# The last output projections as block products, with wo's sums on GpSimd and the first gate and up weights loaded earlier

## The chip, the cores and the metric

The kernel runs on one core of one Trainium2 chip. The metric is the device time of one execution in microseconds (us). The kernel before has a median of 749.18 us over three runs (748.45 to 749.22).

## The reference

x is 2048 tokens by 1024 features, all tensors are bf16. It is normalised, goes through a linear attention block and a SwiGLU block, and the two are joined as x + s * silu(f).

```python
xn = _layernorm(x, axis=-1)
# linear attention, 32 heads of 32
q, k, v = split_heads(xn @ wqkv)
phi = lambda t: jnp.where(t > 0, t + 1, jnp.exp(t)) + 1e-6
pq, pk = phi(q), phi(k)
kv = jnp.einsum("bhsd,bhse->bhde", pk, v)
z = jnp.einsum("bhsd->bhd", pk)
o = jnp.einsum("bhqd,bhde->bhqe", pq, kv) / (jnp.einsum("bhqd,bhd->bhq", pq, z)[..., None] + 1e-6)
s = merge_heads(o) @ wo
# SwiGLU, inner width 3584
f = (silu(xn @ w_gate) * (xn @ w_up)) @ w_down
return x + s * silu(f)
```

## The kernel before, in words

All matrix products take 128 partitions and 512 moving columns at a time. There are four stages on TensorE's queue.

1. The front (to 154 us of the span): normalisation, transposes, keys, values, most of the queries, and the sums kvz over the tokens.
2. The output stage (154 to 233 us), in which the change lies. The 2048 tokens are 4 blocks (b) of 4 tiles (t) of 128 tokens. For each tile `emit_ND` multiplies pqT (phi of the queries, one tile for each pair of feature groups) with KVZ, eight matmuls of 132 columns into three PSUM buffers of pool psA; VectorE adds to the denominators (L794), inverts them (L797) and multiplies (L800) into o_sb. `emit_OT` writes o_sb to HBM from ScalarE's queue and reads it back transposed from SyncE's (SP's) queue into oT; blocks 0 and 1 have oT of their own (`oT_ab`), blocks 2 and 3 lie in wq_sb (`oT_cd`), which is free by then. `emit_S` is one unit: eight matmuls oT x wo for one tile and one half (cc) of the 1024 output columns, into one of five PSUM buffers (pool psB); ScalarE copies it to s_sb, and after the second half s_sb is stored to s_dram.
3. Gate and up (233 to 580 us). Each weight group is 256 columns wide. A product of 2x2 blocks is made as seven block products of half the depth (M1 to M5, N6, N7; `Group` with part_a, part_b, part_c), on sums of blocks that VectorE makes (`sum_w` for the weights, four operations; `xsum_ops` for the activations).
4. Down and the output (580 to 747 us), again by seven block products; the last add of each output tile is GpSimd's (L1193).

Within the output stage the order is written out by hand, with `manual_schedule` for TensorE, VectorE, ScalarE, GpSimd and SP. It is a loop over 32 S units numbered u = 0 to 31, tile by tile and half by half. Sets name the units before which something else is put: `nd_at` the remaining `emit_ND` tiles, `row_at` the `part_d` of the last query groups (VectorE's L190 and L191: phi's last two operations on a row of pqT), `q_at` the last query group's parts. Only the order on each engine is fixed by this; what an engine waits for is found from the data, by the tile framework. GpSimd has no work in this stage. The last part_d stands at u = 9; its row of pqT is read by the eighth matmul of the `emit_ND` of tile (2,0), at u = 10.

When the transpose of the last tile, (3,3), has been issued, `emit_OT` issues the loads of the first three gate and up weight groups (`load_w`, 512 KB each for gate and up). `sum_w(0, 0)` and `sum_w(0, 1)` stand ahead of the last four units.

Of the kernel before, what the change touches and what calls it, by code (L numbers as in the profile page):

```python
# [21 lines left out]
def kernel(  # L22
# [11 lines left out]
    nc = tc.nc  # L34
# [94 lines left out]
    def products(acc, lhs, rhs, n, first, c0=0, c1=CW):  # L129
        for k in range(n):  # L130
            marks["mm"] = nc.tensor.matmul(acc[:, 0:c1 - c0], lhsT=lhs(k), rhs=rhs(k)[:, c0:c1], start=(first and k == 0),  # L131
                                           stop=(k == n - 1), skip_group_check=True)
# [33 lines left out]
    def sum_w(m, gu):  # L166
        wsum[(m, gu)] = ws_all[:, m % 2, gu]
        for op in wsum_ops(wraw[(m, gu)], wsum[(m, gu)]):
            op()
# [41 lines left out]
    class QGroup:  # L211


        def __init__(self, p, m):
            w = wq_sb[:, :, m * FW:(m + 1) * FW]
            self.lhs, self.rhs = block_operands(w, ws_all[:, m // 2, m % 2]), x_operands(p)
            self.out = pqT_tiles[(p, m)]
            self.row = {}

        def mm(self, acc, which, first):  # L220
            products(acc, self.lhs[which], self.rhs[which], HD, first)
# [7 lines left out]
        def part_a(self):  # L229
            self.X = psB.tile([P, CW], FP32, name="qX", tag="B")  # L230
            self.mm(self.X, "M3", True)
            self.u = qtmp.tile([P, CW], FP32, name="qu", tag="qu")
            nc.scalar.copy(out=self.u[:], in_=self.X[:])
            self.Y = psB.tile([P, CW], FP32, name="qY", tag="B")
            self.mm(self.Y, "M4", True)
            nc.vector.tensor_tensor(out=self.u[:], in0=self.u[:], in1=self.Y[:], op=ALU.add)
# [519 lines left out]
    with ExitStack() as p2:  # L756
        wop = p2.enter_context(tc.tile_pool(name="wop", bufs=1, reuse_waits="tile"))
        otp = p2.enter_context(tc.tile_pool(name="p2oT", bufs=1))
        work = p2.enter_context(tc.tile_pool(name="p2work", bufs=2))
        small = p2.enter_context(tc.tile_pool(name="p2small", bufs=2))  # L760
        oT_ab = otp.tile([P, 2, G, TB], BF16, name="oT")
        oT_cd = wq_sb[:].rearrange("p c n -> p (c n)").rearrange("p (b g t) -> p b g t", b=2, t=TB)
        s_tiles = {}
        wo_sb = wop.tile([P, G, D], BF16, name="wo_sb")

        def oT_of(b):
            return (oT_ab[:] if b < 2 else oT_cd)[:, b % 2]

        def emit_KVZ():
            for j in range(NJ):  # L770
                g0 = j * GPT
                ng = min(GPT, G - g0)
                nc.vector.tensor_tensor(out=KVZ[:, g0:g0 + ng, 0:P], in0=kvz_ps[j][:, 0:ng, 0:P],
                                        in1=mask[:, None, :].to_broadcast([P, ng, P]), op=ALU.mult)
                nc.vector.tensor_tensor(out=KVZ[:, g0:g0 + ng, P:P + HPG],
                                        in0=kvz_ps[j][:, 0:ng, P:P + 1].to_broadcast([P, ng, HPG]),
                                        in1=sel[:, None, :].to_broadcast([P, ng, HPG]), op=ALU.mult)

        def emit_ND(b, t):
            r0 = b * TB + t * P  # L780
            p, t0 = r0 // SP_TOK, r0 % SP_TOK
            nds = []
            rden = small.tile([P, G, HPG], FP32, name="rden", tag="rden")
            for j in range(NJ):
                g0 = j * GPT
                ng = min(GPT, G - g0)
                nd_ps = psA.tile([P, GPT, NDW], FP32, name="nd_ps", tag="A")
                for gi in range(ng):
                    g = g0 + gi
                    mm = nc.tensor.matmul(nd_ps[:, gi, :], lhsT=pqT_tiles[(p, g // 2)][:, g % 2, t0:t0 + P],  # L790
                                          rhs=KVZ[:, g, :], start=True, stop=True)
                    if j == 0 and gi == 0 and t == 0:
                        marks[("ND", b)] = mm
                nc.vector.tensor_scalar(out=rden[:, g0:g0 + ng, :], in0=nd_ps[:, 0:ng, P:P + HPG],  # L794
                                        scalar1=EPS, scalar2=None, op0=ALU.add)
                nds.append((g0, ng, nd_ps))
            nc.vector.reciprocal(out=rden[:], in_=rden[:])  # L797
            o_sb = work.tile([P, D], BF16, name="o_sb", tag="o_sb", bufs=4)
            for g0, ng, nd_ps in nds:
                nc.vector.tensor_tensor(  # L800
                    out=o_sb[:, g0 * P:(g0 + ng) * P].rearrange("p (g h e) -> p g h e", g=ng, h=HPG),
                    in0=nd_ps[:, 0:ng, 0:P].rearrange("p g (h e) -> p g h e", h=HPG),
                    in1=rden[:, g0:g0 + ng, :, None].to_broadcast([P, ng, HPG, DH]),
                    op=ALU.mult)
            o_ready.append((b, t, o_sb))

        o_ready = deque()

        def emit_OT():
            while o_ready:  # L810
                b, t, o_sb = o_ready.popleft()
                r0 = b * TB + t * P
                nc.scalar.dma_start(out=o_dram[r0:r0 + P, :], in_=o_sb[:])
                nc.sync.dma_start_transpose(out=oT_of(b)[:, :, t * P:(t + 1) * P], in_=o_dram[r0:r0 + P, :])
                if (b, t) == (NB - 1, TPB - 1):
                    for m in range(PREF):
                        load_w(m)

        def emit_S(b, t, cc):
            oT = oT_of(b)  # L820
            ttok = slice(t * P, (t + 1) * P)
            if (b, t) not in s_tiles:
                s_tiles[(b, t)] = work.tile([P, D], BF16, name="s_sb", tag="s_sb")
            s_sb = s_tiles[(b, t)]
            s_ps = psB.tile([P, CW], FP32, name="s_ps", tag="B")
            for c in range(G):
                mm = nc.tensor.matmul(s_ps[:], lhsT=oT[:, c, ttok], rhs=wo_sb[:, c, cc * CW:(cc + 1) * CW],  # L827
                                      start=(c == 0), stop=(c == G - 1))
                if c == 0:
                    marks[("S", b, t, cc)] = mm  # L830
            nc.scalar.copy(out=s_sb[:, cc * CW:(cc + 1) * CW], in_=s_ps[:])  # L831
            if cc == NCC - 1:
                r0 = b * TB + t * P
                nc.scalar.dma_start(out=s_dram[r0:r0 + P, :], in_=s_tiles.pop((b, t))[:])

        PREF = 3
        units = deque((b, t, cc) for b in range(NB) for t in range(TPB) for cc in range(NCC))
        nds = deque((b, t) for b in range(NB) for t in range(TPB))

        def s_unit():  # L840
            emit_S(*units.popleft())

        def nd_tile():
            if nds:
                emit_ND(*nds.popleft())

        with tc.manual_schedule(engines=FRONT_ORDER | {ET.SP}):

            qb, qc = QGroup(NPASS - 1, NM_Q - 2), QGroup(NPASS - 1, NM_Q - 1)
            for c in range(NCC):  # L850
                nc.sync.dma_start(out=wo_sb[:, :, c * CW:(c + 1) * CW], in_=wo_v[:, :, c * CW:(c + 1) * CW])
            emit_KVZ()
            qa.part_b()
            nd_tile()
            qb.part_a()
            emit_OT()
            qa.part_c()
            nd_tile()
            qb.part_b()
            emit_OT()  # L860
            nd_tile()
            qb.part_c()
            emit_OT()


            rows = deque((grp, i) for grp in (qa, qb, qc) for i in range(2))
            nd_at = {1, 2, 4, 6, 8, 10, 11, 13, 15, 16, 17, 19, 20}
            row_at = {0, 1, 3, 5, 7, 9}
            q_at = {0: qc.part_a, 2: qc.part_b, 3: qc.part_c}
            assert len(nd_at) == len(nds) and len(row_at) == len(rows)  # L870
            u = 0
            while units:
                if u in q_at:
                    q_at[u]()
                if u in nd_at:
                    nd_tile()
                if u in row_at:
                    grp, i = rows.popleft()
                    grp.part_d(i)
                if len(units) == 2 * NCC:  # L880
                    sum_w(0, 0)
                    sum_w(0, 1)
                s_unit()
                emit_OT()
                u += 1
    p12.close()
    ps12.close()

# [371 lines left out]
```

## Time and profile before

| | us |
|---|---|
| median of 3 runs | 749.18 (748.45 to 749.22) |
| the profiled execution | 748.76 |
| its span, first to last instruction | 747.0 |
| TensorE busy | 740.2 |
| VectorE busy | 509.2 |
| ScalarE busy | 273.4 |
| GpSimd busy | 51.2 |
| granted TensorE clock | 0.999 |

An instruction's row gives its start in us from the span's start, its length, the engine (PE TensorE, PEld its weight loads, DVE VectorE, ACT ScalarE, POOL GpSimd, SPq and ACTq the queues that issue transfers), the line, and out<-in by the kernel's names. What stands in square brackets is idle time of that engine just before, and what ended it. Matmuls overlap, so that one is shown longer than its share of the time: the starts of two neighbours tell the pace.

### The profile page before, as it was taken

The page shows a single profiled execution, that of the slowest core. Times are in us where ns is not written, and L with a number is a line of the kernel's source. Part 1 is how long each engine was busy: PE and PEld are TensorE (multiplying, and loading weights), DVE is VectorE, ACT ScalarE, POOL GpSimd, SP SyncE. Part 2 cuts the span into 40 slices and gives each one's busy share as a digit, 9 for nine tenths or more (in the row PEclk, how much of TensorE's full clock was granted, in tenths as well). Part 3 has the DMA queues.
Part 4 walks back from the last instruction along what each step waited for, and adds up shares of the span by engine and source line. Part 5 has one row for each costly group of instructions (what it writes and reads, how often), then busy time and mean ns, then how long its engine had stood idle before and what let it go on. Part 6 is the DMA issues. An engine that isn't in the chain of part 4 may idle for free.

```text
span 747.0 us, 9899 instructions
## 1 busy us (share of the span) xinstructions
PE 740.2 (99%) x3708; PEld 347.8 (47%) x3708; DVE 509.2 (68%) x939; ACT 273.4 (37%) x478; POOL 51.2 (7%) x101
## 2 busy tenths in 40 slices
PE   9999999999999999999999999999999999999997
PEld 4544444455544444444444444444444444444454
DVE  6889896688735767886678867876655744445554
ACT  4444574755234334434343333434342111111111
POOL 3310000000000000000000000000000221121220
PEclk9999999999999999999999999999999999999999
DMA  9756000315799543655336643555879745554200
GB/s 318 253 163 168 1 0 1 113 44 160 195 230 276 148 140 104 185 178 161 103 102 198 190 123 106 152 157 161 260 247 349 291 169 183 183 183 183 85 29 29
DMA packets 132464, 118.09 MB, mean 158 GB/s; under 512 B 33728, under 2 KB 112704, under 8 KB 131136
## 3 DMA queue, kind: packets, MB, share of 16 engines
q1 hardware_dynamic: 127520, 108.68, 46.9%
q10 hardware_dynamic: 4896, 8.78, 3.5%
q8 instruction: 29, 0.48, 0.3%
q14 instruction: 19, 0.16, 0.1%
HBM read 70.52 MB, written 39.58 MB: 147 GB/s over the span
## 4 chain that ended last, share of the span: by engine, by line
PE 97%; DMA 1%; DVE 1%; ACT 0%; issue 0%; ACTq 0%; DVEq 0%
PE X L131 29%; PE Y L131 29%; PE Z L131 10%; PE kv_ps L455 9%; PE s_ps L827 6%; PE qY L131 3%; PE qX L131 3%; PE kY L131 2%; PE kX L131 2%; DMA wg_sb<-in_B_w_gate_dram 1%; PE nd_ps L790 1%; PE kvz L484 1%; PE qZ L131 1%; PE w_ps L493 1%; PE kZ L131 1%; PE tr_ps L411 0%
## 5 line engine op out<-in xcount | busy, mean ns | idle before, releaser
L131 PEld LDWEIGHTS <-ws_all 128*128 128x128 bf16 x1420 | 137.7, 98 | 162.3 <-issue 0.2
L923 DVE TENSOR_TENSOR q<-n,Y 128x512 f32<-128x512 f32 x63 | 43.3, 687 | 106.1 <-PE Y L131 106.1
L131 PEld LDWEIGHTS <-xs 128*128 128x128 bf16 (+1 forms) x736 | 69.6, 98 | 76.5
L1193 POOL TENSOR_TENSOR o_out<-y,xres 128x512 bf16<-128x512 f32 x29 | 35.2, 1213 | 663.3 <-DVE y L1192 663.3
L131 PE MATMUL Y<-xs,ws_all 128*128 128x512 f16 (+3 forms) x308 | 70.3, 360 | 0.0
L131 PE MATMUL X<-xnT,ws_all 128*128 128x512 f16 (+1 forms) x280 | 70.2, 379 | 0.0
L131 PE MATMUL X<-xs,ws_all 128*128 128x512 f16 x224 | 57.5, 379 | 0.0
L131 PE MATMUL Z<-xs,ws_all 128*128 128x512 f16 x224 | 57.5, 379 | 0.0
L131 PE MATMUL Y<-xnT,ws_all 128*128 128x512 f16 x224 | 57.5, 379 | 0.0
L1047 ACT ACTIVATE g<-cg 128x512 bf16<-128x512 f32 x56 | 35.3, 631 | 54.1 <-DVE cg L938 54.0
L929 DVE TENSOR_TENSOR u<-Z,q 128x512 f32<-128x512 f32 x63 | 43.1, 685 | 16.0 <-PE Z L131 15.9
L1047 ACT ACTIVATE g<-X 128x512 bf16<-128x512 f32 x28 | 16.7, 597 | 99.5 <-PE X L131 99.5
L455 PEld LDWEIGHTS <-xnT 128*128 128x128 f16 x320 | 30.7, 98 | 35.8 <-DVE xnT L427 0.5
L919 ACT COPY n<-X 128x512 f32<-128x512 f32 x63 | 36.9, 585 | 28.4 <-PE X L131 27.7
L1072 DVE TENSOR_TENSOR ho<-g,up 128x1024 bf16<-128x1024 bf16 x56 | 38.1, 684 | 0.5
L455 PE MATMUL kv_ps<-wk_sb,xnT 128*128 128x512 bf16 x160 | 37.3, 379 | 0.3 <-DVE xnT L427 0.3
L455 PE MATMUL kv_ps<-wv_sb,xnT 128*128 128x512 bf16 x160 | 36.5, 379 | 0.0
L1192 DVE TENSOR_TENSOR y<-y,s_in 128x512 f32<-128x512 f32 x31 | 22.2, 716 | 20.9 <-ACT y L1186 15.8
L131 PEld LDWEIGHTS <-wg_sb 128*128 128x128 bf16 x224 | 21.9, 98 | 27.1 <-issue 0.8
L131 PEld LDWEIGHTS <-wu_sb 128*128 128x128 bf16 x224 | 21.9, 98 | 26.4
L831 ACT CAST s_sb<-s_ps 128x512 bf16<-128x512 f32 x32 | 18.5, 585 | 40.0 <-PE s_ps L827 36.1
L1186 ACT ACTIVATE y<-X 128x512 f32<-128x512 f32 x8 | 4.8, 597 | 69.7 <-PE X L131 69.7
(179 smaller groups left out, 1132.6 us busy)
## 6 DMA issues: line engine op xcount, KB each, us to landing
h_dram<-ho SPq DMA_DIRECT2D x56, 256.0 KB, 2.6
wg_sb<-in_B_w_gate_dram SPq DMA_DIRECT2D x14, 512.0 KB, 4.1
wu_sb<-in_B_w_up_dram SPq DMA_DIRECT2D x14, 512.0 KB, 4.2
wdr<-in_B_w_down_dram SPq DMA_DIRECT2D x14, 512.0 KB, 4.1
ws_all<-h_dram SPq DMA_DIRECT2D x4, 1792.0 KB, 8.6
wds_dram<-wdsA SPq DMA_DIRECT2D x14, 384.0 KB, 2.7
hp_a<-h_dram SPq DMA_DIRECT2D x3, 1792.0 KB, 8.9
o_dram<-o_sb ACTq DMA_DIRECT2D x16, 256.0 KB, 3.1
```

What stands on the lines that cost most here:

```text
L131: marks["mm"] = nc.tensor.matmul(acc[:, 0:c1 - c0], lhsT=lhs(k), rhs=rhs(k)[:, c0:c1], start=(first and k == 0), stop=(k == n - 1), skip_g ...
L455: mm = nc.tensor.matmul(kv_ps[:], lhsT=xn_tok_ap(i)[:, dc, :], rhs=wkv_ap(c)[:, dc, :], start=(dc == 0), stop=(dc == DC - 1))
L484: nc.tensor.matmul(kvz_ps[j][:, gi, 0:P + 1], lhsT=pk_sb[:, g * P:(g + 1) * P], rhs=v_sb[:, g, 0:P + 1], start=(i == 0 and gi == 0), stop= ...
L827: mm = nc.tensor.matmul(s_ps[:], lhsT=oT[:, c, ttok], rhs=wo_sb[:, c, cc * CW:(cc + 1) * CW], start=(c == 0), stop=(c == G - 1))
L831: nc.scalar.copy(out=s_sb[:, cc * CW:(cc + 1) * CW], in_=s_ps[:])
L919: nc.scalar.copy(out=n[:], in_=self.X[:])
L923: nc.vector.tensor_tensor(out=self.q[:], in0=n[:], in1=self.Y[:], op=ALU.add)
L929: nc.vector.tensor_tensor(out=self.u[:], in0=Z[:], in1=self.q[:], op=ALU.add)
L1047: nc.scalar.activation(out=self.g[:, i, j * TB:(j + 1) * TB], in_=src, func=ACT.Silu)
L1072: nc.vector.tensor_tensor(out=self.ho[:, i], in0=self.g[:, i], in1=self.up[:, i], op=ALU.mult)
L1192: nc.vector.tensor_tensor(out=t[:], in0=t[:], in1=self.s_in[:, i, cs], op=ALU.mult)
L1193: (nc.vector if last and (i, j) != (0, 0) else nc.gpsimd).tensor_tensor(out=self.o_out[:, i, cs], in0=t[:], in1=self.xres[:, i, cs], op=AL ...
```

## The change

The last four token tiles (block 3, units 24 to 31) are no longer multiplied with wo by units. They are taken as two pairs of tiles (`SGroup`): the pair's 256 tokens and wo's 1024 columns make a product of 2x2 blocks, and seven block products of four matmuls stand in place of eight of them.

- wo's five block sums are made by GpSimd, one each at u = 10, 11, 12, 14 and 18, into the parts of oT of blocks 0 and 1 and of ws_all that are no longer read.
- The sums of the pairs' oT blocks are four VectorE operations a pair (`sums`); the first pair's stand at u = 23, the second's behind the first pair's part_a. They are written over oT of blocks 1 and 2 and a part of ws_all.
- `sum_w(0, 0)` stands at u = 22, `sum_w(0, 1)` behind the first pair's part_b.
- s_sb has four buffers in place of two.
- The first gate and up weight group is loaded behind the transpose of tile (3,0), ahead of those of (3,1), (3,2) and (3,3); the second and third stay behind that of (3,3).

```diff
+        PREF = 3
+        load_at = {(NB - 1, 0): (0,), (NB - 1, TPB - 1): range(1, PREF)}
...
                 nc.scalar.dma_start(out=o_dram[r0:r0 + P, :], in_=o_sb[:])
                 nc.sync.dma_start_transpose(out=oT_of(b)[:, :, t * P:(t + 1) * P], in_=o_dram[r0:r0 + P, :])
-                if (b, t) == (NB - 1, TPB - 1):
-                    for m in range(PREF):
+                if (b, t) in load_at:
+                    for m in load_at[(b, t)]:
                         load_w(m)
...
-                s_tiles[(b, t)] = work.tile([P, D], BF16, name="s_sb", tag="s_sb")
+                s_tiles[(b, t)] = work.tile([P, D], BF16, name="s_sb", tag="s_sb", bufs=4)
...
+        w11, w12, w21, w22 = wo_sb[:, 0:HD, 0:CW], wo_sb[:, 0:HD, CW:D], wo_sb[:, HD:DC, 0:CW], wo_sb[:, HD:DC, CW:D]
+        ws_hi = ws_all[:, 1].rearrange("p b c -> p (b c)")
+        wos = [oT_ab[:, 0].rearrange("p (a k) t -> p a k t", a=2)[:, a] for a in range(2)]
+        wos += [ws_hi[:, a * HD * CW:(a + 1) * HD * CW].rearrange("p (k c) -> p k c", k=HD) for a in range(2)]
+        wos += [oT_ab[:, 1, 0:HD]]
+        wo_sums = deque((out, u, v, op) for out, (u, v, op) in zip(wos, (
+            (w12, w22, ALU.subtract), (w21, w11, ALU.subtract), (w11, w22, ALU.add), (w21, w22, ALU.add),
+            (w11, w12, ALU.add))))
+        s_rhs = {"M3": wos[0], "M4": wos[1], "M1": wos[2], "M5": w22, "M2": w11, "N7": wos[3], "N6": wos[4]}
...
+        class SGroup:
...
+            def sums(self):
+                o, sm, tt = self.o, self.sum, nc.vector.tensor_tensor
+                a, b = slice(0, P), slice(P, 2 * P)
+                tt(out=self.s1, in0=o[:, 0:HD, a], in1=o[:, HD:DC, b], op=ALU.add)
+                tt(out=sm[:, :, 0:2 * P], in0=o[:, 0:HD, :], in1=o[:, HD:DC, :], op=ALU.add)
+                tt(out=sm[:, :, 2 * P:3 * P], in0=o[:, HD:DC, b], in1=o[:, HD:DC, a], op=ALU.subtract)
+                tt(out=sm[:, :, 3 * P:4 * P], in0=o[:, 0:HD, a], in1=o[:, 0:HD, b], op=ALU.subtract)
...
+            def store(self, i):
+                r0 = ((NB - 1) * TPB + self.t + i) * P
+                nc.scalar.dma_start(out=s_dram[r0:r0 + P, :], in_=self.s[i][:])
+
+            def part_a(self):
...
+                self.mm(self.X, "M3", True)
+                self.u = qtmp.tile([P, CW], FP32, name="qu", tag="qu")
+                nc.scalar.copy(out=self.u[:], in_=self.X[:])
+                self.Y = psB.tile([P, CW], FP32, name="sY", tag="B")
+                self.mm(self.Y, "M4", True)
+                nc.vector.tensor_tensor(out=self.u[:], in0=self.u[:], in1=self.Y[:], op=ALU.add)
+
+            def part_b(self):
+                Z = psB.tile([P, CW], FP32, name="sZ", tag="B")
+                self.mm(Z, "M1", True)
+                nc.vector.tensor_tensor(out=self.u[:], in0=self.u[:], in1=Z[:], op=ALU.add)
+                self.mm(self.X, "M5", False)
+                nc.scalar.copy(out=self.out(0, 1), in_=self.X[:])
+                self.mm(self.Y, "M2", False)
+                nc.scalar.copy(out=self.out(1, 0), in_=self.Y[:])
+
+            def part_c(self):
+                for acc, which, i in ((self.X, "N7", 0), (self.Y, "N6", 1)):
+                    self.mm(acc, which, False)
+                    nc.vector.tensor_tensor(out=self.out(i, i), in0=self.u[:], in1=acc[:], op=ALU.subtract)
+                    self.store(i)
...
             row_at = {0, 1, 3, 5, 7, 9}
+            wo_at = {10, 11, 12, 14, 18}
+            sum_at = {22: lambda: sum_w(0, 0), 23: lambda: groups[0].sums()}
...
-                if len(units) == 2 * NCC:
-                    sum_w(0, 0)
-                    sum_w(0, 1)
+                if u in wo_at:
+                    out, a, b, op = wo_sums.popleft()
+                    nc.gpsimd.tensor_tensor(out=out, in0=a, in1=b, op=op)
+                if u in sum_at:
+                    sum_at[u]()
                 s_unit()
                 emit_OT()
-                u += 1
+            sg, sh = groups
+            sg.part_a()
+            sh.sums()
+            sg.part_b()
+            sum_w(0, 1)
+            sh.part_a()
+            sg.part_c()
+            sh.part_b()
+            sh.part_c()
```

HD is 4 (half of the eight 128-row chunks), CW 512, P 128. `products` issues the HD matmuls of one block product.

More of the change, by code (lines that the diff above doesn't have):

```diff
@@ L834, in emit_S @@
                 nc.scalar.dma_start(out=s_dram[r0:r0 + P, :], in_=s_tiles.pop((b, t))[:])
-        PREF = 3
+        w11, w12, w21, w22 = wo_sb[:, 0:HD, 0:CW], wo_sb[:, 0:HD, CW:D], wo_sb[:, HD:DC, 0:CW], wo_sb[:, HD:DC, CW:D]
[3 more added lines that the diff above has]
+        wos += [oT_ab[:, 1, 0:HD]]
@@ new lines @@
+        wo_sums = deque((out, u, v, op) for out, (u, v, op) in zip(wos, (
+            (w12, w22, ALU.subtract), (w21, w11, ALU.subtract), (w11, w22, ALU.add), (w21, w22, ALU.add),
+            (w11, w12, ALU.add))))
+        s_rhs = {"M3": wos[0], "M4": wos[1], "M1": wos[2], "M5": w22, "M2": w11, "N7": wos[3], "N6": wos[4]}
+        o_sum1 = [ws_hi[:, 2 * HD * CW:2 * HD * CW + HD * P].rearrange("p (k c) -> p k c", k=HD),
+                  oT_cd[:, 0, 0:1].rearrange("p a (k c) -> p (a k) c", k=HD)]
@@ new lines, with __init__, mm, out @@
+        o_sums = [oT_ab[:, 1, HD:DC], oT_cd[:, 0, HD:DC]]
+        class SGroup:
+            def __init__(self, t):
+                self.t = t
+                o = oT_of(NB - 1)[:, :, t * P:(t + 2) * P]
+                a, b = o[:, :, 0:P], o[:, :, P:2 * P]
+                self.o, self.s1, self.sum = o, o_sum1[t // 2], o_sums[t // 2]
+                s1, sm = self.s1, self.sum
+                self.lhs = {"M3": lambda k: a[:, k, :], "M4": lambda k: b[:, HD + k, :],
+                            "M5": lambda k: sm[:, k, 0:P], "M2": lambda k: sm[:, k, P:2 * P],
+                            "M1": lambda k: s1[:, k, :], "N7": lambda k: sm[:, k, 2 * P:3 * P],
+                            "N6": lambda k: sm[:, k, 3 * P:4 * P]}
+            def sums(self):
[5 more added lines that the diff above has]
+                tt(out=sm[:, :, 3 * P:4 * P], in0=o[:, 0:HD, a], in1=o[:, 0:HD, b], op=ALU.subtract)
+            def mm(self, acc, which, first):
+                products(acc, self.lhs[which], lambda k: s_rhs[which][:, k, :], HD, first)
+            def out(self, i, j):
+                return self.s[i][:, j * CW:(j + 1) * CW]
+            def store(self, i):
+                r0 = ((NB - 1) * TPB + self.t + i) * P
+                nc.scalar.dma_start(out=s_dram[r0:r0 + P, :], in_=self.s[i][:])
+            def part_a(self):
+                self.s = [work.tile([P, D], BF16, name="s_sb", tag="s_sb", bufs=4) for _ in range(2)]
+                self.X = psB.tile([P, CW], FP32, name="sX", tag="B")
+                self.mm(self.X, "M3", True)
[17 more added lines that the diff above has]
+                    self.store(i)
@@ L868 @@
             row_at = {0, 1, 3, 5, 7, 9}
+            wo_at = {10, 11, 12, 14, 18}
+            sum_at = {22: lambda: sum_w(0, 0), 23: lambda: groups[0].sums()}
             q_at = {0: qc.part_a, 2: qc.part_b, 3: qc.part_c}
             assert len(nd_at) == len(nds) and len(row_at) == len(rows)
-            u = 0
-            while units:
+            n7 = TPB * NCC
+            groups = [SGroup(t) for t in range(0, TPB, 2)]
+            for u in range(len(units) - n7):
                 if u in q_at:
```

## The prediction

> **What bounds the kernel now.** I read the page's busy shares first, then the chain of waits in order of time, then the order of time of single engines around the change, and last the landings of the transfers there.
>
> ```profile
> PE 740.2 (99%) x3708; PEld 347.8 (47%) x3708; DVE 509.2 (68%) x939; ACT 273.4 (37%) x478; POOL 51.2 (7%) x101
> ```
>
> TensorE has no time to spare, so the change is worth what it takes from TensorE's queue, less any wait that it puts there. GpSimd is idle from 52 to 588 us. In the stretch that is changed the chain reads:
>
> ```profile
> 212.94 9.49 PE s_ps L827 x44
> 222.42 10.90 DMA wg_sb<-in_B_w_gate_dram
> 233.88 1.08 ACT s_sb L831 x2
> 235.00 1.02 PE Y L131 x4
> ```
>
> The 10.90 is not a wait of TensorE: it runs 96 matmuls without a gap from 212.78 to 233.49 (0.216 us each). Its one hole is behind the first four gate matmuls, from 233.49+0.86=234.35 to 235.00: 0.65 us, in which Y's PSUM buffer is still held by a copy of S that waited for a full s_sb. So the old tail counts as if the gate product started at 233.49+0.65=234.14. Now VectorE and TensorE at the place where GpSimd gets work:
>
> ```profile
> 189.85 0.42 DVE L190 TENSOR_SCALAR e_t<-e_t 128x1024 bf16<-128x1024 bf16 x1
> 190.37 0.69 DVE L191 TENSOR_TENSOR pqT<-e_t,pqT 128x1024 bf16<-128x1024 bf16 x1
> 191.62 0.46 DVE L794 TENSOR_SCALAR rden<-nd_ps 128x12 f32<-128x12 f32 x3 [0.56 <-PE nd_ps L790]
> ```
>
> ```profile
> 191.25 0.63 PE L790 MATMUL nd_ps<-KVZ,pqT 128*128 128x132 bf16 x8
> ```
>
> The two VectorE operations are the last part_d. Their result is the operand of the eighth of the matmuls at 191.25 (0.058 us apart, so it is due at 191.66); it is ready at 191.06, 0.6 us ahead. Last, how the two engines get on where both read SBUF, in the down stage:
>
> ```profile
> 588.11 2.02 DVE L1157 TENSOR_TENSOR xs<-ws_all 128x3584 bf16<-128x3584 bf16 x1
> 588.32 2.81 POOL L1193 TENSOR_TENSOR o_out<-y,xres 128x512 bf16<-128x512 f32 x1 [544.27 <-DVE y L1192]
> 590.04 1.65 DVE L1192 TENSOR_TENSOR y<-y,s_in 128x512 f32<-128x512 f32 x1
> 591.61 0.68 DVE L938 TENSOR_TENSOR y<-u,X 128x512 f32<-128x512 f32 x1
> 591.76 1.16 POOL L1193 TENSOR_TENSOR o_out<-y,xres 128x512 bf16<-128x512 f32 x1 [0.63 <-DVE y L1192]
> ```
>
> The GpSimd sum lasts 1.16 us alone. Begun beside L1157, it ends 1.0 us after L1157 does: it stood still until then. L1192, next on VectorE, takes 1.65 instead of 0.68 us and ends 0.55 us behind the sum: it stood still in its turn. So when both read two operands from SBUF, one waits for the other's whole instruction, and the one that waited goes next. L938, with one operand in PSUM, is not touched. L190 is of the kind that blocks too: at 25.15 a one-column GpSimd operation beside it takes 0.42 instead of 0.19 us.
>
> **Block products.** Two pairs of token tiles: 2 x 7 products of 4 matmuls are 56 in place of 64, so 8 x 0.216 = 1.73 us less of TensorE. Of what they bring along, ScalarE's 8 copies of S become 6; VectorE gets 8 operations of 0.69 us (as L923's) and 8 operand sums, priced as the four of sum_w of the same shapes (0.42, 0.68, 0.42, 0.42), 9.4 us in all, where it worked 6.8 of 22 us (the windows, 212 to 234). Their cost lies in the order they stand in, which is counted below.
>
> **Four s_sb tiles.** They remove the 0.65 us hole, since the copies no longer wait for stores that the weight loads slow down. Together 2.38 us off, if nothing comes up.
>
> **Weights sooner.** The first pair (1 MB) is issued at 211.4 instead of 221.2, behind the transpose of tile (3,0) and ahead of those of (3,1), (3,2), (3,3). By issue and time to landing the four transposes land at 215.8, 219.6, 221.0 and 222.9. SP's queue works in order: the six weight loads of before land at 227.3, 231.0, 233.3, 235.2, 236.9, 238.9, so about 1.9 us each once they run, 3.8 for the pair. The DMA engines are full there (share 1.10, 1.08, 1.09, 0.90 in the four 3 us stretches from 210 on). I put (3,1) 3.3 us later, at 222.9, as the gaps take up some; the ends are 0 (all in gaps: 219.6) and 8.1 us, what the first pair of before took (231.0-222.9). The block products also ask for it earlier: M4, the second product, is due at 219.69+0.86=220.55, where the old order first read (3,1) two units later. TensorE then stands 222.9-220.55=2.35 us, between 0 and 7. Behind M4 eleven products and the gate's start follow: 222.9+13x0.864=234.1. A second chain hangs on (3,3): the sums of the second pair wait for it on VectorE, and behind them stand, in order, u+Z of the first pair (0.69), the up weights' sums (1.7), u+Y (0.69) and two subtractions (1.37); ScalarE holds the first pair's stores for these, and behind the stores the copy that product N7 waits for: 1.7+0.7+1.7+0.7+1.4+0.4+0.6=7.2 us, then two products, 8.9 in all. With (3,3) 3 us later, at 225.9, that is 234.8; 3.0 is my estimate from the same loads. So the tail ends at 234.1 to 234.8 against 234.14: between 2.4 us gained and, say, 2 lost, I take 0.2 lost.
>
> **wo's sums on GpSimd.** Five sums of 128x2048. From the two rows of GpSimd's adds, 512 columns 1.156 and 256 columns 0.667 us, the slope is 1.91 ns a column and the sum 0.18+2048x0.00191=4.1 us; in proportion 4.6. [...] I take 4.3, as these rows differ in size alone. They stand at units 10, 11, 12, 14 and 18 in the text, but GpSimd's queue is its own and empty: the first waits only for the last read of block 0's oT, the fourth matmul of the eighth S unit, which ends at 186.63, and for L191 of the part_d before, which holds SBUF to 187.14. It runs to 191.4, and L190, due at 189.85, stands for it; L190 then runs to 191.85, the second sum takes its turn, as it waited while L191 waited for L190's result, and runs to 196.2; L191 ends at 196.9. TensorE needs it at 191.66 and has nothing else it may do: 5.2 us of standing, 4.9 with 4.1, 5.8 with 4.6 and 3.5 with 2.3. All that follows on TensorE, VectorE and the queues moves along, so nothing of it is hidden. The third and later sums meet no VectorE operation of that kind, and end before M3 needs them (212 against about 225).
> [...]
>
> **The sum.** -1.73-0.65+2.35 and the second chain's part make +0.2; with 5.2 it is +5.4 us. The profiled execution took 748.76 us (span 747.0 and 1.8 around it), 0.4 under the median, so 748.76+5.4=754.2, and 754.6 on the median's footing. The likeliest case's own range is 752 to 757.
>
> **Rivals.**
> *GpSimd keeps SBUF through its queue* (0.20): L190 comes in behind more than one sum. For: the memsets at 0.24 to 0.34 us start 0.03 us apart and last 0.10, so GpSimd issues ahead. Against: at 590.04 the waiting engine came next. Each further sum costs 4.3: 758.9 with one, 763.3 if all four go first (204.3+1.1-191.66=13.8).
> [...]
> *L190 and L191 slip in together* (0.12): then only the first sum costs. L191 ends at 192.5, 0.9 us late: 750.3.
> *The sums do not hold VectorE up* (0.20), because GpSimd starts after 191 or gives way. Then the tail alone counts, and the sign is decided by when (3,1) and (3,3) land: with the pair in the queue's gaps nothing stands and it is 746.8; break-even is (3,1) at 222.9 and (3,3) at 225.2; 2 us later than that is 751.2. I give half of this to faster.
> That the earlier load brings nothing of itself is in all cases: the weights' first use by VectorE (12.40 us of waiting) held nobody up, as TensorE had no hole there.
>
> **How the numbers follow.** Forecast 0.48, rivals 0.20, 0.12, 0.20. A measurement of this kernel can tell about 0.2%, 1.5 us. Faster by more: half of the third rival, 0.10. Within: 0.06 of it and 0.08 of the second. Slower: 0.04 of each and the rest, 0.76. Range 748.0 to 760.0: it leaves out the better part of the third rival (0.09) and the first's long end (0.10).
>
> **What would show it.** Right: GpSimd's first sum from about 187 to 191.4; L190 or L191 of the last part_d as an instruction of several us; one hole of TensorE of about 5 us inside the eight matmuls that stood at 191.25; then a hole of about 2 us before sY, ended by the transpose of (3,1). Wrong: VectorE's two operations at 0.42 and 0.69 us, or sums far from 4 us; no hole at sY, and the pair landed before 218. All else, 56 matmuls 0.216 apart and no hole behind the gate's first four, is common to the cases.

## The result, and the profile after

The changed kernel takes 757.96 us (median of 4 runs, 756.46 to 758.87) against 748.82 us for the kernel before on the same chip: ratio 1.0121, 95% interval 1.0108 to 1.0133, so 9.1 us slower where 5.4 were forecast. The profiled execution took 757.7 us, span 755.9, 8.9 us more than before; the gate's first product starts at 242.93, where the old tail counted as if it started at 234.14, so 8.8 of the 8.9 us lie ahead of it. 757.96 lies within 748 to 760, but above the 757 at which the likeliest case's own range ends.

The line of busy shares of the changed kernel (engine, busy us, share, instructions):

```profile
PE 741.7 (98%) x3700; PEld 347.9 (46%) x3700; DVE 522.6 (69%) x955; ACT 272.5 (36%) x476; POOL 72.2 (10%) x106
```

TensorE has eight matmuls fewer and yet 1.5 us more busy time: some of its matmuls must have become slower. The chain of waits shows where (start, us, what):

```profile
190.08 1.42 DVE e_t L190
191.60 4.36 DVE pqT L191
196.29 3.20 PE s_ps L829 x8
...
215.27 7.30 DMA o_dram<-o_sb
222.58 7.54 DMA wq_sb<-o_dram
230.17 1.89 PE sY L131 x4
232.06 1.54 PE sZ L131 x4
```

Before, the first of these stretches of the chain was TensorE's alone, and in the second TensorE ran without a gap (212.78 to 233.49). Now there are two detours: the last part_d on VectorE, and the store of tile (3,1) with its transpose. Behind each, products that take 1.73 (S) and 0.86 us elsewhere take 3.20, 1.89 and 1.54. GpSimd and VectorE in order of time:

```profile
186.91 8.49 POOL L959 TENSOR_TENSOR oT<-wo_sb 128x2048 bf16<-128x2048 bf16 x2 [142.72 <-PE s_ps L829]
195.36 8.51 POOL L959 TENSOR_TENSOR ws_all<-wo_sb 128x2048 bf16<-128x2048 bf16 x2
```

```profile
190.00 1.49 DVE L190 TENSOR_SCALAR e_t<-e_t 128x1024 bf16<-128x1024 bf16 x1
191.60 4.35 DVE L191 TENSOR_TENSOR pqT<-e_t,pqT 128x1024 bf16<-128x1024 bf16 x1
```

L190 (0.42 us before) ends 0.3 us behind the first sum, which ends at 191.21; L191 (0.69 before) ends 0.55 us behind the second, at 195.40. TensorE, in two views of its order of time:

```profile
191.39 0.57 PE L790 MATMUL nd_ps<-KVZ,pqT 128*128 128x132 bf16 x7
196.00 0.29 PE L790 MATMUL nd_ps<-KVZ,pqT 128*128 128x132 bf16 x1 [4.04 <-DVE pqT L191]
196.09 3.41 PE L829 MATMUL s_ps<-wo_sb,oT 128*128 128x512 bf16 x8
```

```profile
225.45 1.03 PE L131 MATMUL sX<-oT,wq_sb 128*128 128x512 bf16 x4
230.17 1.89 PE L131 MATMUL sY<-oT,wq_sb 128*128 128x512 bf16 x4 [3.69 <-DMA wq_sb<-o_dram]
231.85 1.74 PE L131 MATMUL sZ<-ws_all 128*128 128x512 bf16 x4
233.43 1.03 PE L131 MATMUL sX<-wo_sb,oT 128*128 128x512 bf16 x4
```

The eighth nd matmul (one of `emit_ND`'s) starts 4.20 us late (196.00 instead of 191.39+7x0.058=191.80). sY, due at 225.45+0.86=226.31, starts 3.86 us late. (The profile's idle time in brackets, 4.04 and 3.69, is smaller, as it counts from the recorded end of the matmul before; holes are counted by starts here, and by the bracket where the text below gives no starts.) Why the matmuls behind both holes are slow is read from the windows, cut to the records' own stretches (window, length, PE busy and matmuls, PEld, DVE, ACT, POOL, then the granted clock, DMA share, GB/s):

```profile
192.33:195.74 3.41, 0.00 (x0) 0.00 (x0) 3.41 (x1) 0.00 (x0) 3.41 (x2) 1.00 0.64 173
195.74:199.16 3.42, 3.16 (x9) 1.24 (x10) 2.24 (x8) 0.00 (x0) 3.42 (x1) 0.50 0.10 21
```

For 3.41 us the granted clock is 0.50, and matmuls start 0.427 instead of 0.216 us apart; the same happens from 229.88 to 233.29. The sum of the changed kernel is therefore: first hole 4.20, slow matmuls behind it 1.5, second hole 3.86, slow matmuls behind it 1.5, together 11.1; less 1.73 and 0.65 is 8.7, and 8.8 were measured (0.14 of it, 191.39 against 191.25, already ahead of the first hole).

### The profile page after: what moved, and what is told of

The parts are those of the page before. It is cut to its first block, busy times and chain, and to the rows that moved or that the text cites. A ratio compares the mean times of both kernels' runs of the same rounds, so it can differ in the third digit from the quotient of the medians.

```text
span 755.9 us, 9926 instructions
## 1 busy us (share of the span) xinstructions
PE 741.7 (98%) x3700; PEld 347.9 (46%) x3700; DVE 522.6 (69%) x955; ACT 272.5 (36%) x476; POOL 72.2 (10%) x106
## 4 chain that ended last, share of the span: by engine, by line
PE 95%; DMA 2%; DVE 2%; ACT 0%; issue 0%; ACTq 0%; DVEq 0%
PE X L131 29%; PE Y L131 28%; PE Z L131 10%; PE kv_ps L455 9%; PE s_ps L829 4%; PE qY L131 3%; PE qX L131 3%; PE kX L131 2%; PE kY L131 2%; DMA wq_sb<-o_dram 1%; PE kvz L484 1%; DMA o_dram<-o_sb 1%; PE qZ L131 1%; PE nd_ps L790 1%; PE sY L131 1%; PE kZ L131 1%
## 5 line engine op out<-in xcount | busy, mean ns | idle before, releaser
L829 PE MATMUL s_ps<-wo_sb,oT 128*128 128x512 bf16 x128 | 30.9, 393 | 0.0
```

## The experiments

Line numbers move by a few between these kernels (wo's sums stand at L959 to L962, the first operand sum of a pair at L871 or L872); the names of tiles do not. The profiled executions differ by up to 1 us already in the start of sX where no hole lies upstream of it (219.81 to 220.73), so differences under 1 us between the starts of two profiles are not read.

**before_sums**: the kernel before with only the first two sums.

```
+                if u in (10, 11):
+                    ...   # wo's sums for M3 and M4, as in the change
+                    nc.gpsimd.tensor_tensor(out=oT_ab[:, 0]..., in0=a, in1=b, op=ALU.subtract)
```

> The kernel before with the first two of wo's sums added on GpSimd at units 10 and 11 (their results are read by nobody). Theory (the sums alone make the first hole): L190 ends with the first sum, L191 with the second, TensorE stands 4.0 us at the eighth nd matmul, and the granted clock is 0.50 for one stretch of 3.41 us behind it, 1.5 us more: 749.05+5.5=754.6. Rival (in the kernel before, the later wait on a full s_sb takes up part of it, or the transposes run ahead during the hole): under 753.

Measured 754.40 us, ratio 1.0081 (1.0066 to 1.0096), +5.5.

```profile
196.14 0.29 PE L790 MATMUL nd_ps<-KVZ,pqT 128*128 128x132 bf16 x1 [4.04 <-DVE pqT L191]
```

The hole is the same to 0.01 us without any of the rest of the change, and the granted clock fell for one stretch of 3.41 us. So the sums alone cost 5.5 us in the median and 5.3 in the profile, 0.3 of which lie ahead of them. The rest is 4.20 of hole by the starts and 1.5 of half clock, less the 0.65 us hole behind the gate's first four matmuls, which is gone here (the second product starts at 240.27, 0.86 behind the first): that much of the rival is true.

**sums_later**: all five sums behind unit 15, N6's first.

```
+        wo_sums.rotate(1)
...
-            wo_at = {10, 11, 12, 14, 18}
+            wo_at = {16, 17, 18, 19, 20}
```

> The changed kernel with wo's five sums in another order (N6's first) and from unit 16 on, so that the first has to wait for the last read of block 1's oT, some 12 us behind the last part_d. Theory 1 (a GpSimd sum of 4.3 us holds SBUF against the last part_d, and that alone makes the first hole): L190 and L191 take 0.42 and 0.69 us again, the hole of 4.04 us at the eighth nd matmul is gone, and with it the eight matmuls at half the granted clock behind it (0.427 instead of 0.216 us apart, 1.5 us). The second hole (3.86 us and 1.6 us of slow matmuls behind it) stays. 757.96-4.04-1.5=752.4. Rival (GpSimd's 21 us of reading wo_sb slow VectorE and TensorE wherever they stand): the time moves along with the sums and stays at 757 or more.

Measured 752.97, ratio 1.0047 (1.0029 to 1.0065), where 752.4 was expected. The first hole is gone, but the number fits in part by luck: the second hole did not stay as it was, as the last sums now meet sum_w(0,0).

```profile
218.27 1.57 DVE L152 TENSOR_TENSOR ws_all<-wg_sb 128x512 bf16<-128x512 bf16 x1 [2.93 <-DMA wg_sb<-in_B_w_gate_dram]
219.76 4.54 DVE L153 TENSOR_TENSOR ws_all<-wg_sb 128x1024 bf16<-128x1024 bf16 x1
```

L152 came in behind the fourth sum (to 219.56), L153 (0.68 us alone) behind the fifth (to 223.75). The second hole was 2.23 us before sY and 0.92 before sZ, and the clock stayed at 0.50 for two stretches. The rival falls: beside the first three sums (203.46 to 215.55), which meet no VectorE operation of two SBUF operands, S products kept their 1.73 us (as from 204.62 to 206.35).

**sums_split**: each sum as four instructions, at the old places.

```
-                    nc.gpsimd.tensor_tensor(out=out, in0=a, in1=b, op=op)
+                    for k in range(HD):
+                        nc.gpsimd.tensor_tensor(out=out[:, k, :], in0=a[:, k, :], in1=b[:, k, :], op=op)
```

> The changed kernel with each of wo's sums as four instructions of 512 columns, at the same places in the text. Theory 1 (the lock lasts for one instruction of the other engine): L190 and L191 are each held up by at most one piece, about 1.1 us, so L191 ends at about 193 instead of 195.95, the first hole is 1 to 2 us instead of 4.04, and as it is short the granted clock stays at 1.00 behind it, though GpSimd still reads wo_sb beside the matmuls: 757.96-2.5-1.5=754. Rival for the lock (GpSimd keeps SBUF through its queue): L190 or L191 waits for four pieces or more, and the time stays at 757 or more. Rival for the slow matmuls (GpSimd's reads of wo_sb slow TensorE's reads of it): matmuls 0.43 us apart are seen beside the pieces as well.

Measured 752.00, ratio 1.0037 (1.0024 to 1.0050), single runs from 749.20 to 753.61.

```profile
190.19 0.46 DVE L190 TENSOR_SCALAR e_t<-e_t 128x1024 bf16<-128x1024 bf16 x1
190.75 1.46 DVE L191 TENSOR_TENSOR pqT<-e_t,pqT 128x1024 bf16<-128x1024 bf16 x1
```

L191 waited 0.77 us for one piece, and TensorE lost 0.3 us there (the next S starts at 192.33 instead of 192.06), where a hole of 1 to 2 us was expected. GpSimd reads wo_sb for 23 us beside matmuls 0.216 us apart, so the slow matmuls do not come from GpSimd's reads. What is left of the 3 us is the second hole: TensorE stood 3.15 us before sY, with one stretch at 0.50 behind it.

**loads_late**: all weight loads behind (3,3), and sum_w(0,0) next to sum_w(0,1).

```
-        load_at = {(NB - 1, 0): (0,), (NB - 1, TPB - 1): range(1, PREF)}
+        load_at = {(NB - 1, TPB - 1): range(PREF)}
...
-            sum_at = {22: lambda: sum_w(0, 0), 23: lambda: groups[0].sums()}
+            sum_at = {23: lambda: groups[0].sums()}
...
+            sum_w(0, 0)
             sum_w(0, 1)
             sh.part_a()
```

> The changed kernel with all first weight loads behind the transpose of (3,3), as before, and sum_w(0,0) put next to sum_w(0,1), where its weights will have landed. Theory 1 (the 1 MB pair ahead of the transpose of (3,1) makes the second hole): (3,1) lands where it did before, 219.6, moved by the first hole's 6 us, 225.6 against a need at 226.3; the hole of 3.86 us before sY and the 1.6 us of slow matmuls behind it are gone: 757.96-5.5=752.5. Rival (the block products ask for (3,1) two units earlier than the old order, and its store alone already took 7.3 instead of 4.7 us): a hole of 2 us or more stays before sY, and with the sums behind it the time is 755 or more.

Measured 754.99, ratio 1.0076 (1.0059 to 1.0092); the profiled execution, the slowest of four, took 757.34.

```profile
227.23 1.03 PE L131 MATMUL sY<-oT,wq_sb 128*128 128x512 bf16 x4
```

The hole before sY is gone: (3,1) landed at 225.90 against this need. Theory 1 holds for the cause, but not for the size: VectorE, whose order the program fixes, now waited until 233.16 for the weights, which landed at 233.14, and the second pair's u+Y stood behind their eight sums to 236.50; holes of 1.21 and 1.27 us came up before the second pair's M2 and N7, 2 us of them in one stretch, and with them a second stretch at 0.50.

**before_load**: the kernel before with the first pair of weights behind (3,0).

```
-                if (b, t) == (NB - 1, TPB - 1):
-                    for m in range(PREF):
+                if (b, t) in load_at:
+                    for m in load_at[(b, t)]:
...
+        load_at = {(NB - 1, 0): (0,), (NB - 1, TPB - 1): range(1, PREF)}
```

> The kernel before with the first pair of weights loaded behind the transpose of (3,0) instead of (3,3); S and its order unchanged. Theory (the pair delays (3,1) by 5 to 6.5 us, to about 224.5 to 226, and TensorE stands until it lands): the old order first reads (3,1) at 223.15 instead of M4's 220.55, so the hole is 1.3 to 3 us, with 1.5 us of half clock behind it if it fills most of a 3.41 us stretch: 750.3 to 753.6. The prediction's own size (3,1) at 222.9 would give no hole, 749 or a little less.

Measured 751.66, ratio 1.0041 (1.0024 to 1.0058), single runs from 749.19 to 756.06. The profiled run took 750.82; the slower ones have no profile. Not as expected: (3,1) landed at 222.31, in time for the old order, which first reads it at 223.79 here (223.15 before), and there was no hole there. The cost lies elsewhere:

```profile
237.03 1.02 PE L131 MATMUL Y<-xs,wg_sb 128*128 128x512 f16 x4 [1.87 <-ACT s_sb L831]
```

The hole behind the gate's first four matmuls, 0.65 us before by the starts, is 2.03 (237.03 instead of 235.00), as S's stores were held up more (from issue to landing 5.4 us in the median of those from 208 to 234, 4.5 before). So as far as these profiles go, the second hole of the changed kernel needs both halves of the change: the pair ahead of (3,1) in the queue, and M4, which asks for (3,1) 2.6 us sooner than the old order.

**both**: sums in pieces behind unit 15, and loads late, with the edits of sums_later, sums_split and loads_late.

> The changed kernel with both undone: wo's sums in pieces of 512 columns from unit 16 on, N6's first, and all weight loads behind (3,3) with sum_w(0,0) beside sum_w(0,1). What is left of the change are the block products and the four s_sb tiles. Theory 1 (the two holes and their slow matmuls are the whole loss): no hole of TensorE over 0.7 us between 185 and 245, 748.8-1.73-0.65=746.4, at most 1.2 more where a piece holds up the first pair's sums. Rival (the block products themselves cost more than they save, by VectorE's operand sums in the chain): a hole stays before M1 or M5, and the time is 749 or more.

Measured 752.22, ratio 1.0042 (1.0027 to 1.0057), where 746.4 to 747.6 was expected. One operation of VectorE, of 0.41 us, did this:

```profile
218.02 7.77 DVE L872 TENSOR_TENSOR ws_all<-wq_sb 128x512 bf16<-128x512 bf16 x1 [2.16 <-DMA wq_sb<-o_dram]
```

```profile
225.85 1.89 PE L131 MATMUL sZ<-ws_all 128*128 128x512 bf16 x4 [3.34 <-DVE ws_all L872]
```

The first pair's operand sum stood until the last piece of GpSimd had ended, at 225.51, past seven pieces: the prediction's first rival, in another place.

**later_split**: sums_later with the pieces of sums_split.

> The kernel sums_later with its sums in pieces of 512 columns. In the run both, L872 stood 7.4 us beside seven pieces that followed one another, while in sums_split L190 and L191 each came in behind one piece. Theory A (which engine comes next hangs on the operation of VectorE): sum_w(0,0)'s first operation, L152, at about 218.3 comes in behind one piece, 1.0 us. Theory B (a GpSimd queue that has run for long keeps SBUF to its end): L152 stands until the last piece has ended, at about 223.7, over 5 us.

One run, 754.28 us.

```profile
218.27 7.05 DVE L152 TENSOR_TENSOR ws_all<-wg_sb 128x512 bf16<-128x512 bf16 x1 [2.90 <-DMA wg_sb<-in_B_w_gate_dram]
```

The same L152 that came in behind a whole sum in sums_later stood beside pieces to the end of GpSimd's queue (225.04). Theory A falls; the next two runs are on B.

**split_probe** and **split_probe2**: sums_split with three more operations of VectorE, whose results nobody reads, beside the pieces.

```
+                if u in (12, 14, 16):
+                    nc.vector.tensor_tensor(out=...[:], in0=grp.out[:, 0, :], in1=grp.out[:, 1, :], op=ALU.add)
```

> The run sums_split with three more operations on VectorE, each adding two 128x1024 bf16 tiles in SBUF (0.69 us alone), at units 12, 14 and 16, beside pieces 5 to 16 of wo's sums. In sums_split L190 and L191 came in behind one piece each, in later_split L152 stood through six pieces to the end of the queue. Theory B (GpSimd keeps SBUF once its queue has run for some pieces): the first probe may come in behind one piece, a later one stands through all that are left, up to 10 us. Theory C (the hand-over is a race whose outcome belongs to the kernel and its place, with the pieces at 1.145 us the one way and at 1.16 us the other): all three come in behind one piece, 1.0 to 1.8 us each.

> The run split_probe with smaller probes: at units 12 and 16 the operands are four strips of 128 columns apart, as in L152, at unit 14 they are 512 columns in one run; 0.42 us alone. In split_probe all three probes of 1024 columns in one run came in behind one piece; in later_split L152 (four strips) stood through six. Theory A (the form of VectorE's operation decides): the first and third probe stand through the queued pieces, the first 8 us or more, the second comes in behind one piece. Theory D (the form doesn't decide; what stood in later_split and both hangs on something of that place): all three come in behind one piece, under 1.6 us each.

One run each, 750.51 and 749.57 us. The first probe of the first run:

```profile
196.89 1.49 DVE L962 TENSOR_TENSOR probe<-pqT 128x1024 bf16<-128x1024 bf16 x1
```

The other two took 1.35 and 1.12 us, those of the second run 1.23, 0.82 and 1.42. All six, also those of four strips, came in behind one piece, though up to 17 pieces had run: B and the second run's A fall. Why GpSimd kept its turn in two kernels stays open. One thing goes with it: where VectorE came in, GpSimd's next instruction started at most 0.044 us before the recorded end of the one before; in the 12 hand-overs that VectorE lost (six each in the runs both and later_split) it was 0.048 to 0.058. What sets this lead was not tried, so it is not shown to be the cause.

**clean**: sums of 2048 columns behind the last part_d, loads late, weights' sums where they were meant to hold up nobody.

```
+                if u == min(wo_at):
+                    last = grp.out[:, i, 0:1]
+                    nc.gpsimd.tensor_tensor(out=...[:], in0=last, in1=last, op=ALU.add)   # tile wo_go
...
             sg.part_c()
+            sum_w(0, 0)
             sh.part_b()
             sh.part_c()
+            sum_w(0, 1)
```

> The changed kernel with a one-column GpSimd operation ahead of wo's sums that reads the result of the last part_d, so that all five sums stand between 191.1 and 212, where VectorE has no operation with two operands in SBUF; all weight loads behind (3,3), sum_w(0,0) behind the first pair's last subtraction and sum_w(0,1) behind everything. What is left are the block products and four s_sb tiles. Theory (the GpSimd collisions, the transpose behind the weights and VectorE's order were the whole loss): no hole of TensorE over 0.7 us between 185 and 245, granted clock 1.00 throughout, 749.05-1.73-0.65=746.7. Rival (the block products' operand sums cost more than 2.4 us of their own): a hole of 1 us or more before one of the second pair's products, 749 or more.

Measured 747.69, ratio 0.9988 (0.9978 to 0.9997): faster than both kernels, by 1.2 us (interval 0.2 to 1.6) than the kernel before, where 2.4 were expected. `last` is a column of what the last L191 writes.

```profile
191.51 0.20 POOL L959 TENSOR_TENSOR wo_go<-pqT 128x1 bf16<-128x1 bf16 x1 [147.19 <-DVE pqT L191]
```

```profile
PE Y L131 <- DVE q L1014: 0.5, 1, 0.5
```

The second view, TensorE's waits from 180 to 262 us, has one line. L190 and L191 are back at 0.42 and 0.69 us, the clock is 1.00 throughout, and the 0.65 us hole is not gone but has moved before the gate's fifth product, which waits for a VectorE that is busy with weights' sums. By the starts, as the 0.65 was counted, it is 0.67 there (236.22 instead of 234.69+0.86=235.55). So the 1.73 of the eight matmuls remain; the two spans differ by 1.4, and 0.27 of the difference lies ahead of all this (the eight nd matmuls start at 191.52 instead of 191.25).

**clean2**: clean with sum_w(0,1) next to sum_w(0,0), ahead of the second pair's part_b.

> The run clean with both of the up and gate weights' sums, sum_w(0,0) and sum_w(0,1), between the first pair's last subtraction and the second pair's part_b, so that VectorE reaches q=n+Y of the first gate product sooner. Theory: the hole of 0.50 us that clean still had before the gate's fifth product goes, and nothing else comes up: 747.69-0.5=747.2. Rival (the sums now hold up u+Z and the subtractions of the second pair, and with them the copies and PSUM buffers): a hole before sX or before the gate's first four products instead, 747.7 or more.

Measured 748.25, ratio 0.9992 (0.9983 to 1.0000): the hole before the gate's fifth product grew from 0.50 to 0.76 us instead of going. This order of VectorE's sums brought no gain.

**clean_s2**: clean with two s_sb tiles.

```
-                ... tag="s_sb", bufs=4) ...
+                ... tag="s_sb") ...
```

> The run clean with two s_sb tiles again instead of four. Theory (the four tiles are worth the 0.65 us hole and no more): a pair's part_a needs two tiles whose stores have landed; the copies into them come back to waiting for stores, and a hole of 0.5 to 2 us appears in the second pair or at the gate's first products: 748.2 to 749.7. Rival (with the loads behind (3,3) the stores land in time and two tiles do): 747.7, as clean.

Measured 753.53, ratio 1.0064 (1.0049 to 1.0080).

```profile
233.93 1.86 PE L131 MATMUL sX<-ws_all,wq_sb 128*128 128x512 bf16 x4 [3.60 <-ACT s_sb L901]
```

The hole is 3.60 us where 0.5 to 2 were expected, and two stretches at 0.50 came with it. The second pair's first copy waits for the store of the first pair, issued at 227.68 beside the weight loads and landed at 233.21. With two tiles the block products cost 5.8 us more: a pair fills two tiles at once, so in this kernel the four tiles are a condition of the block products and not a gain beside them.

## Why the prediction was right, and where its sizes were off

**wo's sums on GpSimd, +5.2.** Right in every step: L190 blocked by the first sum, VectorE's turn, L191 by the second, TensorE standing in the eighth nd matmul with nothing else to do; before_sums shows that it is the sums alone, sums_split that VectorE waited there for one instruction of GpSimd (L191, 0.77 us). The term came out at 4.20 us: a sum takes 4.06 where nothing touches it (the fifth, from 208.75), as the slope's 4.1 had it, not 4.3; L190 and L191 needed 0.28 and 0.55 us behind the hand-over, not 0.42 and 0.69; and the matmul was due 0.14 us later. The prediction's 3.5 us of standing is worked out from 2.3 us for a sum, which no run shows: with both operands bf16 it was these 4.06 us. Nor does the proportion's 4.6 hold.

**Weights sooner, +2.35 and the second chain.** The place (before sY) and its releaser (the transpose of (3,1)) are right, loads_late shows the cause, and the range of 0 to 7 held it. The mis-sized step is "I put (3,1) 3.3 us later": taking off the 5.76 us by which sX itself started later, (3,1) landed at 224.4 instead of 219.6, 4.7 later. The step left out the store ahead of the transpose, which ran beside the same pair and took 7.3 instead of 4.7 us; the transpose then took 7.5 instead of 5.4, landing 1.2 us behind the pair's second half (228.88). How the delay splits is not fixed: in the six other kernels with the pair ahead of (3,1) the store took 3.5 to 5.8 us and the transpose 7.1 to 9.0. From the store's issue to the transpose's landing these seven kernels took 12.2 to 14.9 us, and the seven without the pair there 7.5 to 10.1. Against the 10.1 of the kernel before the pair thus cost 2.0 to 4.7 us: the forecast 3.3 lies inside, and the changed kernel's profile shows the long end. Behind M4 stand twelve products, not eleven; 13x0.864 counts M4 and these twelve, so that the sum stands. The second chain, by (3,3), did not decide: no hole before N7. In loads_late, where VectorE waited for the weights instead, a chain of its kind did.

**What was missing.** The sum took a hole for its own length. Each of the two also cost 1.5 us of half clock: about 3.0 of the 3.4 us by which 5.4 and 8.8 differ. The rest is -1.0 (first hole), +1.5 (second) and -0.2 (the second chain's part). That these nearly cancel is luck; the forecast came out 3.4 us low because the clock had no term in it.

**Block products and s_sb tiles, -2.4.** The eight matmuls are gone (56 in place of 64), and in the changed kernel there is no hole behind the gate's first four. By themselves they are worth 1.2 us in clean (1.4 by the spans), about half of the forecast, since VectorE's new work brings the 0.65 us hole back, as 0.67, at another product.

**The rivals.** "GpSimd keeps SBUF through its queue" did not happen in the changed kernel, where VectorE came in at once after each sum; but a VectorE operation did stand to the end of the queue in two other kernels, L872 for 7.77 us in both and L152 for 7.05 in later_split. L190 and L191 did not slip in together, and VectorE was held up, so the second and third rival are out.

## What to carry to other kernels

A slack of 0.6 us on one engine can be lost to a queue that looks idle, as here, where L190 took 1.49 instead of 0.42 us and L191 4.35 instead of 0.69: before work goes to GpSimd, look at which VectorE operations with two SBUF operands (or a plain tensor-scalar in SBUF) run while it is there, and give its first instruction something to wait for that lies behind them, as one column of the last result did in clean. A load that is moved ahead in a queue can delay the transfers behind it and the stores beside it (here by 2.0 to 4.7 us), and the price is decided by who asks first for the delayed one: M4, due at 226.31, started 3.86 us late in the changed kernel, while S, reading at 223.79 in before_load, lost nothing. A forecast of a long wait of TensorE needs a term for the clock behind it, an estimated 1.5 us, which is what each stretch at 0.50 cost in the changed kernel: holes of 2.23 us (sums_later) to 4.20 us brought such a stretch, those of 2.27 us in split_probe and 2.03 in before_load did not.

## What the runs showed of the hardware

**The granted clock went by stretches of 3.41 us.** In the changed kernel's records it is 1.00 for 191.146, 30.720 and 522.239 us ahead of its three drops (at 195.74, 229.88 and 755.53), which are 56, 9 and 153 times 3.413, and 0.50 for 3.413 us behind each of the first two; in the kernel before it is 1.00 for 740.692 us, 217 times 3.413, ahead of its only drop, at the end. In sums_later it was 0.50 for two such stretches (224.22 to 231.05). What came next went with TensorE's busy time within the stretch. Two stretches of loads_late with the first hole cut in two, and the one behind them:

```profile
191.24:194.66 3.42, 1.52 (x13) 0.78 (x10) 3.32 (x2) 0.59 (x2) 3.42 (x2) 1.00 0.74 219
194.66:198.07 3.41, 1.23 (x6) 0.66 (x8) 3.17 (x6) 0.00 (x0) 3.41 (x2) 1.00 0.35 77
198.07:201.48 3.41, 3.41 (x16) 1.76 (x14) 2.48 (x9) 0.58 (x1) 3.41 (x2) 0.50 0.21 77
```

Behind 1.52 us of work the clock stayed at 1.00, behind 1.23 it fell. Other stretches at full clock agree: those with 1.54 us of work (before_load) and 1.69 (split_probe2) were followed by full clock, those with 1.43 (loads_late), 1.18 (sums_later), 0.66 (clean_s2), 0.58 (sums_split) and 0.00 (the changed kernel) by half. At 0.50, stretches with 2.50 us (sums_later) and 2.57 (clean_s2) were followed by another at 0.50, those with 2.92 (loads_late) and 2.93 (both) by full clock. A hole of 2.27 us that fell across two stretches in split_probe brought no drop,

```profile
219.22:222.63 3.41, 2.28 (x11) 0.84 (x9) 0.36 (x2) 1.49 (x3) 0.00 (x0) 1.00 1.16 264
222.63:226.04 3.41, 2.27 (x11) 1.09 (x12) 2.22 (x5) 0.00 (x0) 0.00 (x0) 1.00 1.08 243
```

while 2.23 us within one stretch in sums_later brought a stretch at 0.50, and the 0.92 us in that one a second.

**Whose turn it was.** VectorE operations with two operands in SBUF, and L190, were seen to stand behind whole instructions of GpSimd: in the changed kernel L190 (0.42 us alone) ended at 191.49, 0.28 us behind the first sum, and L191 0.55 us behind the second; in sums_later L152 and L153 took 1.57 and 4.54 us instead of 0.42 and 0.68. Mostly VectorE came in next: L190 in the changed kernel stood between the first sum and the second, which ended at 195.40, and L191 in sums_split, 0.69 us alone, ended 0.55 us behind the piece that it waited for, so, counted back, it began 0.14 us ahead of that piece's recorded end. In the runs both and later_split it did not: L872 in both, 0.41 us alone and waiting since 218.02, took 7.77 us and lost six turns to pieces that started later.
